# Three pairs of tiles transposed in 64-row halves, with the compute queues in a new order

## The chip, the cores and the metric

The kernel runs on one core of a Trainium2 chip. The metric is the device time of one execution in microseconds. TensorE multiplies into PSUM, which has eight banks; ScalarE and VectorE read PSUM, GpSimd does not; DMA queues are fed here from SyncE (SP). In profile lines the engines are PE (TensorE), PEld (its weight loads), ACT (ScalarE), DVE (VectorE), POOL (GpSimd) and SP.

## The reference

One transformer block on x of 2048 tokens and 448 features, all in bf16: a layer norm, an attention that is linear in the tokens ("hedgehog": softmax of plus and minus a learned projection as feature map), a residual, a second layer norm and a gated unit.

```
h  = x + A(layernorm(x));  out = h + B(layernorm(h))

A: q, k, v = split(x @ wqkv)                       # 16 heads of 28
   pq, pk = q @ w_phi, k @ w_phi                   # per head, 28 x 28
   phi(p) = concat(softmax(p), softmax(-p))        # 56 features
   kv  = sum over tokens of phi(pk)^T v;  z = sum over tokens of phi(pk)
   o   = (phi(pq) @ kv) / (phi(pq) . z + 1e-6)
   return o @ wo                                   # 448 x 448
B: return (sigmoid(x @ w_gate) * (x @ w_up)) @ w_down   # 448 -> 1792 -> 448
```

## The kernel before, in words

The 2048 tokens are 16 tiles of 128. Partition p of tile t holds token 16p + t, so a tile is one slice of `x_sb`. A matmul contracts over partitions, so three times a tile has to be turned so that features lie on partitions: the normed x (`xT`, into `xnT`), the attention's o (`oT`, into `oT`), and the normed h (`hT`, into `hnT`, which is the same memory as `xnT`). For most tiles a DMA transpose on SP's queue does it. For the tiles that come first in each stage TensorE does: x tiles 0 to 3, o tiles 0 and 1, h tiles 0 and 1. `pe_transpose` makes four 128 x 128 transposes of a tile into one bank (the 448 features lie in 512 padded columns), and `evac` copies the bank out on ScalarE or VectorE. Such an op is named `xT2`, its copy `xT2e`.

The contraction of 448 is done as seven blocks of 64 rows. Two 64-row halves of TensorE's array work at once, one for each of two banks (`pair`, `both`); after the first four steps (op `...a`) the halves change banks for the last three (op `...b`). The `a` and `b` op of one pair write the same banks from different halves, and where nothing lies between them the `b` op waits for the `a` op to end (`Graph.crosses`). Whole 128-row work is left in the warm-up multiplies (`warm0` to `warm9`), the folding of the weights (`wT`, `w2m`), these transposes, and the last down projections (`dm`).

The stages, in the order of time:

1. x arrives; statistics `bst`, `agg`; reciprocal root `pow1`; normed tile `xn`; its transpose `xT`. The weight fold for K (`w2m0`) and later for Q (`w2m1`, its copies `w2e1`).
2. For each tile: K features and V (`pva`, `pvb`; for tiles 0 to 3 `vva`, `vvb`, `ppa`, `ppb`, two tiles at a time), exponentials `ek` and V copy `v1_t` on ScalarE, the sums `ss`, their reciprocals `rs` and the products `phi` on VectorE or GpSimd, and the accumulation `kva`, `kvb` into banks 6 and 7. In between, Q features of the first chunk (`pqa`, `pqb`, exponentials `eq`; a chunk is four tiles).
3. `kvz` copies the accumulated kv out. `num` multiplies a tile's Q features with it; `rsm`, `qq`, `b`, `c`, `rden` on VectorE, `o` on GpSimd or VectorE; `oT`; the output projection `woa`, `wob`; the residual `h`; statistics (`bs2`, `ag2`, `pow2` for the first two tiles, `sq`, `ve`, `pow2` for the others); `hn`; `hT`.
4. The gates and ups (`ga`, `gb`; ScalarE `sig`, VectorE `hh`), two tiles at a time for tiles 0 to 3 and four at a time ("wide") from tile 4 on, and the down projections (`dn`, `dp`, later `dm`), `fin`, `out`. The attention of the later tiles runs among them.

The order of every engine is written out by hand in `ORDER`, one list of op names for each of sp, act, pe, dve and pool. Each engine executes its list in that order. Which engine executes an op that could run on several (`evac`, `xn`, `phi`, `o`, `hn`, `ve`, `nm`, `kvz`) follows from the list that holds its name. `Graph` finds from the keys that an op reads and writes (tiles, banks) which semaphores it has to wait for. `PROGRAM` sets only the order in which ops are declared.

Line 309 of the profile is the multiply in `both`, line 538 the transposes in `pe_transpose`, line 531 the copies in `evac`, line 612 the weight fold in `fold`, lines 671 and 672 the two exponentials in `ekv` (their tile `ek` lies in the memory of `hhT` and stands in the profile under that name), line 721 the exponentials in `pq`.

Of the kernel before, what the change touches and what calls it, by code (L numbers as in the profile page):

```python
# [18 lines left out]
class Graph:  # L19
# [90 lines left out]
    def emit(self, nc):  # L110
# [85 lines left out]
P = 128  # L196
# [5 lines left out]
KT = 4  # L202
# [123 lines left out]
def build(nc, A_x, A_wqkv, A_w_phi, A_wo, B_w_gate, B_w_up, B_w_down, out):  # L326
# [10 lines left out]
    with ExitStack() as es:  # L337
# [66 lines left out]
        def TS(t):  # L404
            return slice((t % 4) * P, (t % 4 + 1) * P)
# [126 lines left out]

        def pe_transpose(name, srcs, bank, dst, rkey, wkey):
            ps = bk16(bank)[:, 0:512]

            def f(e):
                for kt, src in enumerate(srcs):
                    p = e.transpose(ps[:, kt * P:(kt + 1) * P], src, ident[:])  # L538
                return p
            op("pe", name, f, r=["ident", rkey], w=[B(bank)])  # L540
            evac(name + "e", dst, ps.rearrange("p (k s) -> p k s", k=KT), B(bank), wkey)
# [22 lines left out]
        def xnorm(t, a):  # L564
            s = t % NX
            src = windows(x_sb[:, t, :])
            dst = xn_pad[:, s, :].rearrange("p (a f) -> p a f", a=2)

            def fa(e):
                return e.activation(dst, src, ACT.Identity, bias=nb1[:, t:t + 1], scale=rst1[:, t:t + 1])  # L570

            def fd(e):
                return e.tensor_scalar(dst, src, mv1[:, t, 0:1], rst1[:, t:t + 1], op0=ALU.subtract, op1=ALU.mult)

            def fp(e):
                return e.tensor_scalar(dst, src, nm1[:, t:t + 1], rst1[:, t:t + 1], op0=ALU.add, op1=ALU.mult)
            need = {"act": ("nb1", a), "pool": ("nm1", a), "dve": ("mv1", t)}[Graph.engine("xn%d" % t)]
            op(("act", "dve", "pool"), "xn%d" % t, (fa, fd, fp), r=[("x", t), ("rst1", a), need], w=[("xn", s)])
            if t < 4:
                pe_transpose("xT%d" % t, [xn_pad[:, s, kt * P:(kt + 1) * P] for kt in range(KT)], 6 + t % 2,  # L580
                             xnT[0][:, :, TS(t)], ("xn", s), ("xnT", t))
            else:
                op("sp", "xT%d" % t, lambda e: e.dma_start_transpose(out=xnT[t // 4][:, :, TS(t)], in_=xn_pad[:, s, :]),
                   r=[("xn", s)], w=[("xnT", t)], dma="tr", nring=64)
# [67 lines left out]
        def proj(t):  # L652
            bp, bv = t % 2, 2 + t % 2
            pairop("pva%d" % t, "pvb%d" % t, pair(bk(bp)[:, 0:D], bk(bv)[:, 0:D], x(t), x(t), wk2, wv),
                   [("xnT", t)] + W2k + wv_keys, bp, bv)

        def proj2(nm, t, b, w, r):
            pairop("%sa%d" % (nm, t), "%sb%d" % (nm, t), pair(bk(b)[:, 0:D], bk(b + 1)[:, 0:D], x(t), x(t + 1), w, w),
                   [("xnT", t), ("xnT", t + 1)] + r, b, b + 1)
# [51 lines left out]
        def pq(c, i, b):  # L711
# [3 lines left out]
            r = W2q + [("xnT", 4 * c + j) for j in range(4)]  # L715
# [101 lines left out]
        def otrans(t):  # L817
            so = t % NO
            if t < 2:
                pe_transpose("oT%d" % t, [o_pad[:, so, kt * P:(kt + 1) * P] for kt in range(KT)], 2 + t % 2, oT[:, so, :, :],  # L820
                             ("opad", so), ("oT", so))
            else:
                op("sp", "oT%d" % t, lambda e: e.dma_start_transpose(out=oT[:, so, :, :], in_=o_pad[:, so, :]),
                   r=[("opad", so)], w=[("oT", so)], dma="tr", nring=64)

        def resid(t, b, ha=False):
# [28 lines left out]
            if t >= 2:  # L855
                op("sp", "hT%d" % t, lambda e: e.dma_start_transpose(out=hnT[c][:, :, TS(t)], in_=hn_pad[:, s, :]),
                   r=[("hn", s)], w=[("xnT", t)], dma="tr", nring=64)

        def htrans(t):
            s = t % NH  # L860
            pe_transpose("hT%d" % t, [hn_pad[:, s, kt * P:(kt + 1) * P] for kt in range(KT)], t, hnT[0][:, :, TS(t)], ("hn", s), ("xnT", t))

        def wout(t):
# [14 lines left out]
            r = [("oT", t % NO), ("oT", (t + 1) % NO)] + wo_keys + ([("x", t), ("x", t + 1), "ident"] if ha else [])  # L878
# [5 lines left out]
        def wout1(t):  # L884
# [5 lines left out]
            r = [("oT", so)] + wo_keys  # L890
# [10 lines left out]
        def gate_up(t0, n, ff):  # L901
# [3 lines left out]
            hk = [("xnT", t) for t in range(t0, t0 + n)]  # L905
# [129 lines left out]
```

## Time and profile before

| | us |
|---|---|
| median of 3 runs | 202.45 (202.28 to 202.48) |
| the profiled execution's own time | 202.7 |
| its span, first to last instruction | 200.8 |
| TensorE busy | 195.5 (97%) |
| VectorE busy | 132.0 (66%) |
| ScalarE busy | 89.4 (45%) |
| GpSimd busy | 56.2 (28%) |

The granted TensorE clock is 1.000 over the whole span. A row of the timeline is: start, length, engine, line, operation, out<-in by the program's names, partitions of weights x columns, shape of the moving operand, how many; in brackets idle time of the engine before it and what ended that. Rows of TensorE overlap, since its multiplies are pipelined; the distance from one start to the next is what a piece of work takes of the engine. In the chain of waits a row is start, length and the work that held the chain. Times are microseconds from the span's start.

### The profile page before, as it was taken

Reading aid. Unit: us, or ns where it says so; the run is one execution under the profiler, and the core shown is the slowest. Engines: PE = TensorE matmul, PEld = TensorE weight load, DVE = VectorE, ACT = ScalarE, POOL = GpSimd, SP = SyncE. Lnnn points to the kernel's source line nnn. Section 1 sums busy time; section 2 is a strip of 40 time slices with the busy share of each in tenths; the row PEclk is TensorE's granted clock in tenths of the full one; section 3 lists DMA queues with packets and bytes.
Section 4 is the critical chain, followed back from the end, with each engine's and each line's share of the span. In section 5 each row is a group of like instructions: output and inputs, shape, how many; then the busy total and the mean of one; then the engine's idle time right before and its main releaser. Section 6 shows DMA issues by size and latency. Waiting matters only on the chain.

```text
span 200.8 us, 5854 instructions
## 1 busy us (share of the span) xinstructions
PE 195.5 (97%) x2516; PEld 114.4 (57%) x2516; DVE 132.0 (66%) x308; ACT 89.4 (45%) x174; POOL 56.2 (28%) x95
## 2 busy tenths in 40 slices
PE   7999999999999999999999999999999999999995
PEld 4835556565568778787444444555555555554443
DVE  5999999978888986576569877346332422272224
ACT  2668988898883451434232432324323212222220
POOL 5779948633343207510170110001400000000000
PEclk9999999999999999999999999999999999999999
DMA  6965346749984230360015220020312000004002
GB/s 157 316 140 129 54 83 76 221 144 302 309 206 66 52 57 15 66 82 3 0 29 124 56 42 10 20 58 26 65 38 52 0 3 2 0 3 137 0 3 91
DMA packets 32490, 16.26 MB, mean 81 GB/s; under 512 B 24720, under 2 KB 31568, under 8 KB 32464
## 3 DMA queue, kind: packets, MB, share of 16 engines
q1 hardware_dynamic: 32336, 15.86, 33.7%
q8 instruction: 20, 0.33, 0.7%
q14 instruction: 6, 0.05, 0.1%
q10 hardware_dynamic: 128, 0.03, 0.1%
HBM read 8.34 MB, written 1.84 MB: 51 GB/s over the span
## 4 chain that ended last, share of the span: by engine, by line
PE 92%; ACT 3%; DMA 2%; issue 1%; SPq 1%; DVE 0%
PE psum L309 84%; PE psum L954 5%; DMA wk_sb<-in_A_wqkv_dram 2%; ACT hhT L671 1%; ACT eq L721 1%; ACT hhT L672 1%; PE psum L524 1%; PE psum L538 1%; PE psum L612 1%; SPq L413 1%; PE psum L599 0%; ACT xnT L531 0%; ACT v L531 0%; DVE x_sb L961 0%
## 5 line engine op out<-in xcount | busy, mean ns | idle before, releaser
L309 PE MATMUL psum<-xnT,wu_sb 64*128 64x512 bf16 (+1 forms) x490 | 93.6, 333 | 0.0
L309 PE MATMUL psum<-xnT,wg_sb 64*128 64x512 bf16 (+1 forms) x490 | 93.5, 333 | 0.1
L925 ACT ACTIVATE sg_sb<-psum 128x512 bf16<-128x512 f32 x56 | 33.2, 596 | 90.1 <-PE psum L309 89.5
L926 DVE SCALAR_TENSOR_TENSOR hhT<-sg_sb,psum 128x512 bf16<-128x512 bf16 x56 | 37.7, 684 | 52.1 <-ACT sg_sb L925 51.7
L309 PEld LDWEIGHTS psum<-xnT,wg_sb 64*128 64x128 bf16 x490 | 44.6, 94 | 20.9 <-DVE hhT L926 2.5
L309 PEld LDWEIGHTS psum<-xnT,wu_sb 64*128 64x128 bf16 x490 | 44.7, 94 | 13.9
L309 PE MATMUL psum<-wd_sb,hhT 64*128 64x448 bf16 x336 | 37.3, 349 | 0.0
L309 PEld LDWEIGHTS psum<-wd_sb,hhT 64*128 64x128 bf16 x336 | 17.8, 94 | 14.2 <-DVE x_sb L836 0.5
L309 PE MATMUL psum<-Wk,xnT 64*128 64x448 bf16 x112 | 22.2, 350 | 0.5 <-ACT hhT L672 0.2
L309 PE MATMUL psum<-wv_sb,xnT 64*128 64x448 bf16 x112 | 22.3, 351 | 0.1
L810 POOL TENSOR_TENSOR o_pad<-c_sb,rden 128x448 bf16<-128x448 bf16 x11 | 10.2, 935 | 28.5 <-DVE rden L806 28.4
L675 DVE TENSOR_REDUCE ss<-hhT 128x32 f32<-128x896 bf16 x16 | 16.8, 1060 | 0.2 <-ACT hhT L672 0.2
L721 ACT ACTIVATE eq<-psum 120x1024 bf16<-120x1024 f32 x16 | 15.6, 1030 | 0.6 <-PE psum L309 0.4
L685 POOL TENSOR_TENSOR phi<-hhT,rs 128x896 bf16<-128x896 bf16 x8 | 13.6, 1710 | 5.6 <-DVE rs L681 3.4
L309 PE MATMUL psum<-xnT,Wq 64*120 64x512 bf16 x112 | 14.8, 383 | 0.3 <-ACT eq L721 0.2
L845 POOL TENSOR_SCALAR ve<-ssq 128x1 f32<-128x1 f32 x11 | 2.2, 201 | 41.8 <-ACT junk L842 41.5
L309 PE MATMUL psum<-wo_o,oT 64*128 64x448 bf16 x56 | 13.2, 350 | 0.0
L309 PE MATMUL psum<-wo_e,oT 64*128 64x448 bf16 x56 | 13.2, 349 | 0.0
L961 DVE SCALAR_TENSOR_TENSOR x_sb<-psum,x_sb 128x448 bf16<-128x448 f32 (+2 forms) x17 | 9.4, 592 | 2.9 <-PE psum L954 1.6
L954 PE MATMUL psum<-wd_sb,hhT 128*128 128x448 bf16 (+2 forms) x70 | 11.2, 316 | 0.0
L309 PEld LDWEIGHTS psum<-Wk,xnT 64*128 64x128 bf16 x112 | 7.8, 94 | 5.8 <-PE psum L309 1.0
L671 ACT ACTIVATE hhT<-psum 128x448 bf16<-128x448 f32 x16 | 8.8, 553 | 4.4 <-PE psum L309 4.2
(105 smaller groups left out, 234.4 us busy)
## 6 DMA issues: line engine op xcount, KB each, us to landing
out_dram<-x_sb SPq DMA_DIRECT2D x15, 112.0 KB, 1.8
x_sb<-in_A_x_dram SPq DMA_DIRECT2D x7, 224.0 KB, 4.2
wd_sb<-in_B_w_down_dram SPq DMA_DIRECT2D x7, 224.0 KB, 5.1
wg_sb<-in_B_w_gate_dram SPq DMA_DIRECT2D x3, 448.0 KB, 5.8
wu_sb<-in_B_w_up_dram SPq DMA_DIRECT2D x3, 448.0 KB, 5.7
wv_sb<-in_A_wqkv_dram SPq DMA_DIRECT2D x2, 224.0 KB, 4.7
wk_sb<-in_A_wqkv_dram SPq DMA_DIRECT2D x2, 196.0 KB, 4.1
wo_e<-in_A_wo_dram SPq DMA_DIRECT2D x1, 336.0 KB, 3.3
```

Of the source, the lines that this page charges most:

```text
L309: p = e.matmul(o, lhsT=w, rhs=r, start=st, stop=sp, tile_position=(row, 0))
L413: return op(eng, name, lambda e: e.dma_start(dst, src), r=r, w=w, dma="in" if eng == "sp" else "ain", nring=48 if eng == "sp" else 8, kb=kb)
L671: e.activation(ek[:, s, :, 0, :], src, ACT.Exp)
L675: op("dve", "ss%d" % t, lambda e: e.tensor_reduce(ss[:, s, :].rearrange("p (b h) -> p b h", h=2), eks.rearrange("p b (d h) -> p b h d", h= ...
L685: return e.tensor_tensor(phi[:, sp, :, :, :].rearrange("p b a n -> p (b a) n")[:, :, 0:56].rearrange("p b (d h) -> p b d h", h=2), eks.rea ...
L721: op("act", "eq%d_%d%s" % (c, i, "pm"[sg]), lambda e, sg=sg: e.activation(eq[c][:, sg, 2 * i:2 * i + 2, :].rearrange("p g n -> p (g n)"), ...
L810: return e.tensor_tensor(o_pad[:, t % NO, off:off + D].rearrange("p (h d) -> p h d", h=H), c_sb[:, t % NS, :, 0:DH], rden[:, t % NS, :][:, ...
L845: op(("pool", "dve"), "ve%d" % t, lambda e: e.tensor_scalar(ve2[:, t:t + 1], ssq2[:, t:t + 1], 1.0 / D ** 3, EPS, op0=ALU.mult, op1=ALU.ad ...
L925: op("act", "sig" + nm, lambda e: e.activation(sg_sb[:, k, 0:W], bk(bg)[:, 0:W], ACT.Tanh, scale=0.5), r=[B(bg)], w=[("sg", k)])
L926: op("dve", "hh" + nm, lambda e: e.scalar_tensor_tensor(out=dst, in0=sg_sb[:, k, 0:W].rearrange("p (f n) -> p f n", n=N), scalar=1.0, in1= ...
L954: p = e.matmul(bk(b)[:, lo:hi], lhsT=hb[:, ff, TS(t)], rhs=wd_sb[:, ff, lo:hi], start=ff == 0, stop=ff == FT - 1)
L961: op("dve", "fin%d%s" % (t, nm), lambda e: e.scalar_tensor_tensor(out=h_sb[:, t, lo:hi], in0=bk(b)[:, lo:hi], scalar=0.5, in1=h_sb[:, t, l ...
```

## The change

Tiles 2 and 3 of x, 0 and 1 of o, and 0 and 1 of h are transposed by one op for each pair (`xT2`, `oT0`, `hT0`), which stands where the second tile was declared. For each of the pair's eight 128 x 128 blocks it issues two transposes of 64 rows, one in each half of the array. The lower half writes one bank, the upper half the other: a bank holds one half of the tokens of both tiles, where it held all tokens of one tile. There are still two copies of 128 x 512 for each pair, which now write runs of 64 elements, and what reads one tile waits for both copies. So that this is tracked, the keys of `xnT` and `oT` are split by half (`XT`, `OT`).

The lists for act, pe, dve and pool have a new order up to about the gates of tiles 4 to 7. SP's list and `PACE` are as before. Ops also change engines: `xT3e` from act to dve, `oT1e` from dve to act, `o1` and `o4` from pool to dve, `o7` and `o8` from dve to pool, `phi8` from pool to dve and `phi5` from dve to pool, `v1_11` for `v1_13` on dve, `kvzA` for `kvzC` on dve, `nm1_6`, `nm1_8`, `nm1_12` from act to pool, `hn2`, `hn3` from dve to pool and `hn7` from pool to dve, and others of `ve`, `nm`, `o`.

```diff
+        def XT(t):
+            return [("xnT", t, 0), ("xnT", t, 1)]
...
+        def pair_transpose(names, srcs, banks, dst, rkeys, wkeys):
+            ps = [bk16(b)[:, 0:512] for b in banks]
+
+            def f(e):
+                for i, tile in enumerate(srcs):
+                    for kt, src in enumerate(tile):
+                        o = slice((i * KT + kt) * 64, (i * KT + kt + 1) * 64)
+                        for h, rows in enumerate((LO, HI)):
+                            p = e.transpose(ps[h][:, o], src[rows], ident[rows, rows], tile_position=(64 * h, 0))
+                return p
+            op("pe", names[0], f, r=["ident"] + rkeys, w=[B(b) for b in banks], rows=64, half={b: h for h, b in enumerate(banks)})
+            for h in range(2):
+                evac(names[h] + "e", dst[h], ps[h].rearrange("p (t k s) -> p t k s", t=2, k=KT), B(banks[h]), [k[h] for k in wkeys])
...
-            if t < 4:
+            if t in (2, 3):
+                if t == 3:
+                    v = xnT[0][:, :, 2 * P:4 * P].rearrange("p k (t h s) -> p h t k s", t=2, h=2)
+                    pair_transpose(("xT2", "xT3"), [[xn_pad[:, u % NX, kt * P:(kt + 1) * P] for kt in range(KT)] for u in (2, 3)], (6, 7),
+                                   [v[:, 0], v[:, 1]], [("xn", 2 % NX), ("xn", 3 % NX)], [XT(2), XT(3)])
...
+                    pair_transpose(("oT0", "oT1"), ..., (2, 3), [v[:, 0], v[:, 1]], [("opad", 0), ("opad", 1)], [OT(0), OT(1)])
...
+                    pair_transpose(("hT0", "hT1"), ..., (0, 1), [v[:, 0], v[:, 1]], [("hn", 0), ("hn", 1)], [XT(0), XT(1)])
```

The parts of the four lists that the prediction speaks of, before and after:

```diff
 act
-"... par ek0 xT3e ek1 v1_0 v1_1 nm1_6 ek2 ek3 v1_2 w2e1_1 v1_3 nm1_8 w2e1_0 v1_4 ek4 ..."
+"... par ek0 ek1 v1_0 v1_1 w2e1_1 ek2 v1_2 ek3 v1_3 w2e1_0 ek4 v1_4 ..."
-"... eq0_1m eq0_1p eq1_0p kvzA kvzB eq1_0m eq1_1p eq1_1m eq2_0m oT0e eq2_0p eq2_1m eq2_1p h1 h0 eq3_0p eq3_0m ..."
+"... eq0_1m eq0_1p eq1_0m kvzB kvzC eq1_0p eq1_1m eq1_1p eq2_0m oT0e oT1e eq2_0p eq2_1p eq2_1m h1 h0 eq3_0m eq3_0p ..."
 pe
-"... ppa0 ppb0 warm9 xT2 xT3 vva0 vvb0 ppa2 ppb2 vva2 seed vvb2 w2m1_0 w2m1_1 kva0 pva4 kvb0 pvb4 pva5 w2m1_2 w2m1_3 pvb5 ..."
+"... ppa0 ppb0 warm9 xT2 vva0 vvb0 ppa2 w2m1_1 ppb2 vva2 seed vvb2 w2m1_3 w2m1_0 pva4 pvb4 kva0 pva5 kvb0 kva1 pvb5 ..."
-"... pvb8 kvb3 pqb0_0 pva9 kva4 pvb9 pva10 kvb4 kva5 pvb10 kvb5 pva11 kva6 pvb11 ..."
+"... pvb8 kva3 pva9 kvb3 kva4 pvb9 pva10 kvb4 kva5 pvb10 kvb5 pva11 pqb0_0 kva6 pvb11 ..."
-"... qs pqa1_1 num0 num1 pqb1_1 pqa2_0 num2 pqb2_0 pqa2_1 oT0 oT1 num3 pqb2_1 woa0 wob0 ... num5 hT1 hT0 woa2 ga0_2 ..."
+"... qs pqa1_1 num0 pqb1_1 num1 pqa2_0 num2 pqb2_0 pqa2_1 oT0 pqb2_1 num3 wwo woa0 wob0 ... num5 hT0 woa2 ga0_2 ..."
 dve
-"... bst5 bst4 xn2 agg5 agg4 agg7 bst6 xT2e agg6 ss0 bst8 rs0 ..."
+"... bst5 agg7 bst4 xn2 agg5 agg4 bst9 bst6 xT3e xT2e agg6 bst11 ss0 bst10 rs0 ..."
-"... rsm2 rden1 qq2 b2 c2 oT1e rsm3 ... rsm5 hT1e qq5 hT0e b5 c5 ..."
+"... rsm2 rden1 qq2 o1 b2 c2 rsm3 ... rsm5 hT0e qq5 hT1e b5 rden4 c5 o4 ..."
 pool
-"... o0 o1 o2 o3 pow2_1 pow2_0 o4 o5 o6 ve2 ..."
+"... o0 o2 o3 pow2_1 pow2_0 o5 o6 ve3 o7 pow2_2 pow2_3 nm2 hn2 hn3 ..."
```

More of the change, by code (lines that the diff above doesn't have):

```diff
@@ L531, in evac, with OT @@
             op(("act", "dve"), name, (lambda e: e.copy(dst, src), lambda e: e.tensor_copy(dst, src)), r=[rkey], w=[wkey])
+        def XT(t):
+            return [("xnT", t, 0), ("xnT", t, 1)]
+        def OT(t):
+            return [("oT", t, 0), ("oT", t, 1)]
+        def pair_transpose(names, srcs, banks, dst, rkeys, wkeys):
[10 more added lines that the diff above has]
+                evac(names[h] + "e", dst[h], ps[h].rearrange("p (t k s) -> p t k s", t=2, k=KT), B(banks[h]), [k[h] for k in wkeys])
         def pe_transpose(name, srcs, bank, dst, rkey, wkey):
@@ L578, in xnorm @@
             op(("act", "dve", "pool"), "xn%d" % t, (fa, fd, fp), r=[("x", t), ("rst1", a), need], w=[("xn", s)])
-            if t < 4:
+            if t in (2, 3):
[3 more added lines that the diff above has]
+                                   [v[:, 0], v[:, 1]], [("xn", 2 % NX), ("xn", 3 % NX)], [XT(2), XT(3)])
+            elif t < 2:
                 pe_transpose("xT%d" % t, [xn_pad[:, s, kt * P:(kt + 1) * P] for kt in range(KT)], 6 + t % 2,
-                             xnT[0][:, :, TS(t)], ("xn", s), ("xnT", t))
+                             xnT[0][:, :, TS(t)], ("xn", s), XT(t))
             else:
                 op("sp", "xT%d" % t, lambda e: e.dma_start_transpose(out=xnT[t // 4][:, :, TS(t)], in_=xn_pad[:, s, :]),
-                   r=[("xn", s)], w=[("xnT", t)], dma="tr", nring=64)
+                   r=[("xn", s)], w=[XT(t)], dma="tr", nring=64)
         for ts in ([0], [1], [2], [3], [4, 5], [6, 7], [8, 9, 10, 11], [12, 13, 14, 15]):
@@ L654, in proj @@
             pairop("pva%d" % t, "pvb%d" % t, pair(bk(bp)[:, 0:D], bk(bv)[:, 0:D], x(t), x(t), wk2, wv),
-                   [("xnT", t)] + W2k + wv_keys, bp, bv)
+                   [XT(t)] + W2k + wv_keys, bp, bv)
         def proj2(nm, t, b, w, r):
             pairop("%sa%d" % (nm, t), "%sb%d" % (nm, t), pair(bk(b)[:, 0:D], bk(b + 1)[:, 0:D], x(t), x(t + 1), w, w),
-                   [("xnT", t), ("xnT", t + 1)] + r, b, b + 1)
+                   [XT(t), XT(t + 1)] + r, b, b + 1)
         def vcopy(t):
@@ L714, in pq @@
                           lambda h, k: xnT[c][h, k, :], lambda h, k: xnT[c][h, k, :])
-            r = W2q + [("xnT", 4 * c + j) for j in range(4)]
+            r = W2q + [XT(4 * c + j) for j in range(4)]
             op("pe", "pqa%d_%d" % (c, i), f1, r=r, w=[B(b), B(b + 1)], rows=64, half={b: 0, b + 1: 1})
@@ L819, in otrans @@
             if t < 2:
-                pe_transpose("oT%d" % t, [o_pad[:, so, kt * P:(kt + 1) * P] for kt in range(KT)], 2 + t % 2, oT[:, so, :, :],
-                             ("opad", so), ("oT", so))
+                if t == 1:
+                    v = oT[:, 0:2, :, :].rearrange("p t k (h s) -> p h t k s", h=2)
+                    pair_transpose(("oT0", "oT1"), [[o_pad[:, u, kt * P:(kt + 1) * P] for kt in range(KT)] for u in (0, 1)], (2, 3),
+                                   [v[:, 0], v[:, 1]], [("opad", 0), ("opad", 1)], [OT(0), OT(1)])
             else:
                 op("sp", "oT%d" % t, lambda e: e.dma_start_transpose(out=oT[:, so, :, :], in_=o_pad[:, so, :]),
-                   r=[("opad", so)], w=[("oT", so)], dma="tr", nring=64)
+                   r=[("opad", so)], w=[OT(so)], dma="tr", nring=64)
         def resid(t, b, ha=False):
@@ L856, in resid @@
                 op("sp", "hT%d" % t, lambda e: e.dma_start_transpose(out=hnT[c][:, :, TS(t)], in_=hn_pad[:, s, :]),
-                   r=[("hn", s)], w=[("xnT", t)], dma="tr", nring=64)
+                   r=[("hn", s)], w=[XT(t)], dma="tr", nring=64)
         def htrans(t):
-            s = t % NH
-            pe_transpose("hT%d" % t, [hn_pad[:, s, kt * P:(kt + 1) * P] for kt in range(KT)], t, hnT[0][:, :, TS(t)], ("hn", s), ("xnT", t))
+            if t == 1:
+                v = hnT[0][:, :, 0:2 * P].rearrange("p k (t h s) -> p h t k s", t=2, h=2)
+                pair_transpose(("hT0", "hT1"), [[hn_pad[:, u, kt * P:(kt + 1) * P] for kt in range(KT)] for u in (0, 1)], (0, 1),
+                               [v[:, 0], v[:, 1]], [("hn", 0), ("hn", 1)], [XT(0), XT(1)])
         def wout(t):
@@ L877, in fb @@
                             xp(t, 2, HI, False) + [(bk(2)[:, 0:D], ot(t)(HI, k), wo_e[HI, k, :], False, k == 2) for k in (0, 1, 2)])
-            r = [("oT", t % NO), ("oT", (t + 1) % NO)] + wo_keys + ([("x", t), ("x", t + 1), "ident"] if ha else [])
+            r = [OT(t % NO), OT((t + 1) % NO)] + wo_keys + ([("x", t), ("x", t + 1), "ident"] if ha else [])
             op("pe", "woa%d" % t, fa, r=r, w=[B(2), B(3)], rows=64, half={2: 0, 3: 1})
@@ L889, in part @@
                 return [(bk(b)[:, 0:D], oT[h, so, k, :], w[h, k, :], first and k == ks[0], not first and k == ks[-1]) for k in ks]
-            r = [("oT", so)] + wo_keys
+            r = [OT(so)] + wo_keys
             op("pe", "woa%d" % t, lambda e: both(e, part(LO, lo, True), []), r=r, w=[B(b)], rows=64, half={b: 0})
@@ L904, in gate_up @@
             ns = slice((t0 % 4) * P, (t0 % 4) * P + N)
-            hk = [("xnT", t) for t in range(t0, t0 + n)]
+            hk = [XT(t) for t in range(t0, t0 + n)]
             two = n == 2
```

65 rows, old and new, of the table ORDER are left out of this document.

## The prediction

> **What bounds the kernel now.** I read the page first, then the chain of waits, then the timeline of one engine at a time around each stall.
>
> ```profile
> span 200.8 us, 5854 instructions
> ```
>
> ```profile
> PE 92%; ACT 3%; DMA 2%; issue 1%; SPq 1%; DVE 0%
> ```
>
> TensorE carries nearly all of the chain that ends last. What an edit is worth is therefore the TensorE time that it takes away or adds, unless another engine makes TensorE wait at that place. The chain of waits (start, length, work) shows where that is so:
>
> ```profile
> 11.34 0.54 ACT hhT L671
> 11.88 0.43 ACT hhT L672
> 12.32 0.48 ACT xnT L531
> 12.79 0.45 ACT hhT L671
> 13.24 0.45 ACT hhT L672
> 13.69 0.14 issue
> 13.82 0.95 PE psum L309 x8
> 14.77 0.05 issue
> ...
> 17.45 0.43 ACT v L531
> 17.89 0.14 issue
> 18.02 2.49 PE psum L309 x30
> ...
> 47.20 1.95 ACT eq L721 x2
> 49.15 0.04 issue
> 49.19 1.07 PE psum L309 x8
> ```
>
> Three restarts of TensorE hang on ScalarE: ppa2 at 13.82 (behind ek0, the copy xT3e, and ek1), pva4 at 18.02 (behind v1_2), pqa2_1 at 49.19 (behind two exponentials). From 18 to 43 and from 59 to the end TensorE is on the chain almost alone. So 11 to 18 and 44 to 59 are the places to follow.
>
> **The transposes themselves.** TensorE's timeline at the three pairs, before:
>
> ```profile
> 11.23 0.29 PE L524 MATMUL psum<-zero 128*128 128x128 bf16 x2
> 11.35 0.61 PE L538 MATMUL psum<-ident,xn_pad 128*128 128x128 bf16 x8
> 11.89 1.74 PE L309 MATMUL psum<-wv_sb,xnT 64*128 64x448 bf16 x14
> ```
>
> ```profile
> 50.20 0.62 PE L538 MATMUL psum<-ident,o_pad 128*128 128x128 bf16 x8
> 50.75 0.40 PE L309 MATMUL psum<-kvz,eq 56*128 56x60 bf16 x16
> 50.99 0.84 PE L309 MATMUL psum<-xnT,Wq 64*120 64x512 bf16 x6
> 51.66 0.35 PE L309 MATMUL psum<-x_sb,ident 64*128 64x448 bf16 x2
> ```
>
> ```profile
> 57.59 0.62 PE L538 MATMUL psum<-ident,hn_pad 128*128 128x128 bf16 x8
> 58.14 0.36 PE L309 MATMUL psum<-wo_e,oT 64*128 64x448 bf16 x1
> ```
>
> Start to start, eight whole transposes and what follows them take 0.54 to 0.55. Two matrix multiplies of the same shape take 0.12 (11.23 to 11.35), at most 0.06 each, so eight take 0.45 to 0.48 and the change to 64-row work some 0.09. I take 0.09 for the change in the other direction too. No row shows a transpose in 64-row halves. The nearest is one `num`: 16 multiplies of 60 columns, alternating between the two row halves, take 0.24 (50.75 to 50.99), 15 ns each. Sixteen half transposes move 64 columns each, so 0.24 is my value and the lower end; the upper end is 16 at a whole transpose's 0.055 (0.44 divided by eight), 0.88. In the two later pairs the neighbours are 64-row work, so both changes of mode go as well: 0.55 + 0.09 - 0.24 = 0.40 of TensorE each. The first pair still stands behind `warm9`, whose rows are whole, and keeps one: 0.54 - 0.09 - 0.24 = 0.21. That is 1.01 us of TensorE. The question is how much of it meets a wait.
>
> The Trainium skill ("TensorE: Matmul & The Clock Gate", the section on 56 against 53.3 ns) says that starts of matmuls never come closer than about 25 ns, however few columns they have. By it a group of 16 takes 0.40 and not 0.24. The row at 50.75 disagrees, at 15 ns, but those are multiplies and not transposes; that case is the second rival.
>
> **Stage 1, 11 to 18 us.** The copy xT3e moves from ScalarE to VectorE, so ek1 ends 0.48 earlier (the L531 row of the chain), and ppa2 can start at 13.82 - 0.48 = 13.34. TensorE is ready then: half transposes 0.09 + 0.24 after 11.35, so the V projection starts at 11.68 instead of 11.89. Its row is 1.74 long, and the next work can start 0.16 before such a row ends (50.75 + 0.40 against 50.99), so 1.58 later, at 13.26. VectorE makes both copies:
>
> ```profile
> 11.78 0.42 DVE L531 COPY xnT<-psum 128x512 bf16<-128x512 bf16 x1
> ```
>
> bst9 now stands ahead of them, so they start about 12.2 and end by 12.2 + 2 x 0.42 = 13.04, before 13.34. Then the query fold w2m1_1 goes between ppa2 and ppb2. It fills the gap in which ppb2 waits for ppa2 to leave the banks: four pairs and the gap take 1.00 (13.82 + 0.95 + 0.05 - 13.82), seven pairs and the gap 1.58, so a pair takes 0.19 and the gap 0.23 to 0.24. The fold costs four multiplies, 0.20, and two changes of mode, 0.18: +0.15 here, taken back later, where one fold less runs. pva4 needs v1_2:
>
> ```profile
> 16.38 0.74 PE L309 MATMUL psum<-wv_sb,xnT 64*128 64x448 bf16 x6
> ```
>
> ```profile
> 17.31 0.57 ACT L531 CAST v<-psum 128x448 bf16<-128x448 f32 x1
> ```
>
> The V block that it reads ends at 16.38 + 0.74 - 0.48 + 0.15 = 16.79. v1_2 now stands ahead of ek3, so it starts with that: 16.79 + 0.04 + 0.57 + 0.14 to issue = 17.54, against 18.02. Stage 1: **-0.48**.
>
> **Stage 2, the K/V tiles to 44 us.** The new order of TensorE moves pqb0_0 and the kv steps so that other work lies in some of the gaps between a projection's two halves (about 0.12 each), and puts ScalarE's v copies closer to their users (I followed each tile's ek and v; three restarts come 0.1 to 0.2 late). I net this at +0.08. The danger is VectorE, which has no room:
>
> ```profile
> 30.00:35.00 5.00, 5.00 (x100) 3.14 (x98) 5.00 (x9) 4.33 (x11) 4.02 (x3) 1.00 0.60 70
> ```
>
> ```profile
> 42.22 1.14 DVE L685 TENSOR_TENSOR phi<-hhT,rs 128x896 bf16<-128x896 bf16 x2
> ```
>
> ```profile
> 43.69 0.76 PE L309 MATMUL psum<-v,phi 64*128 64x58 bf16 x24 [0.15 <-PE psum L309]
> ```
>
> Busy 5.00 of 5.00 (third pair of columns), its last two phi end at 43.36, and the block that uses the last one starts at 43.69. It gets one copy more (0.42, of which 0.08 overlaps). I expect it to win that back, because ek and the aggregates reach it 0.4 earlier and it stops waiting for them; if it wins nothing back, phi ends at 43.70 and stage 2 eats the whole gain (first rival). The moves between VectorE and GpSimd in this stage (phi5 for phi8, v1_11 for v1_13) swap equal shapes; their cover is the same slack of 0.3.
>
> **Stage 3, the o and h pairs, 44 to 59 us.**
>
> ```profile
> 49.99 0.64 DVE L804 TENSOR_TENSOR c_sb<-b_sb,psum 128x464 bf16<-128x464 bf16 x1
> ```
>
> ```profile
> L810 DVE TENSOR_TENSOR o_pad<-c_sb,rden 128x448 bf16<-128x448 bf16 x5 | 3.1, 625 | 0.1
> ```
>
> ```profile
> 50.63 0.58 ACT L531 COPY oT<-psum 128x512 bf16<-128x512 bf16 x1 [0.58 <-PE psum L538]
> ```
>
> In before's clock: num1 (0.24) now follows pqb1_1, so the exponentials of 47.20 start some 0.22 earlier and pqa2_1 starts at 48.97; it took 1.01 up to the transposes, 0.09 of it the change of mode, so it is done by 49.89. The pair waits for o1. o1 now runs on VectorE ahead of b2 and c2, when c1 and the small steps behind it are done at 49.2: 49.2 + 0.63 = 49.83, transposes 0.12 after that at 49.95, pqb2_1 at 50.19 (0.67 long, 50.99 to 51.66). b2 and c2 move by what of o1 their old waits don't absorb, 0.42: c2 ends at 50.63 + 0.42 = 51.05, and num3 waits to 51.18, a stall of 0.3 that was not there. Both copies are ScalarE's, one behind the other: 50.39 + 0.58 + 0.48 = 51.45, and woa0 starts at 51.55 against 51.66: **-0.11**. The 0.40 that the transposes gave up became waiting for the copies and c2.
>
> ```profile
> 55.60 3.77 ACT L721 ACTIVATE eq<-psum 120x1024 bf16<-120x1024 f32 x4
> ```
>
> ```profile
> 58.44 0.42 DVE L531 COPY xnT<-psum 128x512 bf16<-128x512 bf16 x1
> ```
>
> The h pair waits for banks that the second of these exponentials frees. The chain from woa0 to it moves by the same 0.11, so the pair starts at 57.48, and woa2 at 57.72 instead of 58.14. The gates wait for the second VectorE copy, though: it ends at 57.92 + 0.42 + 0.42 = 58.76 where it ended at 58.86. No gain beyond the 0.11.
>
> **Stage 4, after 59 us.** TensorE is full, and steps that change places (num9 to num11, dn0, ga2) do the same work.
>
> ```profile
> 57.48 0.94 POOL L810 TENSOR_TENSOR o_pad<-c_sb,rden 128x448 bf16<-128x448 bf16 x1 [1.08 <-DVE rden L806]
> ```
>
> ```profile
> oT<-o_pad SPq DMA_TRANSPOSE x14, 2.5
> ```
>
> o4, here on GpSimd, goes to VectorE behind c5, about 2 us later; its DMA transpose, and oT5's behind it on SP's queue, leave later too. The cover is sixteen gate steps ahead of woa4. hn2 and hn3 go the other way and delay theirs by about 1 us, with as much cover ahead of ga2_2. If a cover is gone, TensorE stands for the overhang, each landing 2.5 us after its issue. num10's c9 comes close, and I put +0.05 for that.
>
> **The sum.** -0.48 + 0.08 - 0.11 + 0.05 = -0.46. The profiled execution took 202.7 with a span of 200.8, so its own time would be 202.24, the span 200.34. It was 0.25 above the median of 202.45; on the median the forecast is **202.0**, -0.23%.
>
> **Rivals.**
> - *VectorE holds stage 2.* The extra copy isn't won back, kva15 starts no earlier than now, and stages 1 and 2 give nothing: -0.11 + 0.05, 202.4. For it: 5.00 of 5.00. Against: VectorE's own waits in this stage are for data that now come earlier. 0.14.
> - *The two row halves don't overlap, each half costing half a whole:* 16 x 0.0275 = 0.44, 0.20 over my value. The first pair has 0.08 of slack, the other two none: -0.46 + 0.12 + 0.40 = +0.06, 202.5. 0.07; the Trainium skill's floor of 25 ns would end in the same place.
> - *A half costs as much as a whole, one after the other* (the other side): 0.88 a group, 0.64 over. -0.46 + 0.56 + 1.28 = +1.38, 203.8. It decides from 26 ns a half transpose, where nothing is left; from 35 ns the kernel is slower by 0.2%. For it: transposes have only been seen whole, and their 64-row form isn't in this trace. Against: 15 ns in the `num` rows. 0.17, with everything between 35 and 55 ns.
> - *All of the freed TensorE time shows*: -0.48 and twice -0.40, 201.2. Against: the copies and exponentials above. 0.10.
>
> **How the numbers follow.** Forecast 0.52. A measurement of this kernel tells about 0.2% (0.4 us) from no change, and the forecast lies just past that: I put 0.37 of it beyond and 0.15 within. Faster: 0.37 + 0.10 = 0.47. Same: 0.15 + 0.14 + 0.07 = 0.36. Slower: 0.17. The forecast's own range is 201.7 to 202.3. 201.3 to 203.0 takes in the two middle rivals, most of the fast one and the near part of the slow one, and leaves out nearly 0.2.
>
> **What the profile after would show.** Right: 16 half transposes in about 0.24 before the next start; ppa2 at about 13.35, pva4 at 17.5; woa0 and the gates 0.5 earlier than before, with idle time on TensorE ahead of num3 and of the first gate that it did not have. Wrong: a group of 0.44 or more; a K/V block waiting for a phi of VectorE; pva4 no earlier than 17.9; a projection that waits for a DMA transpose; or the first gate 0.9 earlier, which would be the fast rival.

## The result and the profile after

| | before | after |
|---|---|---|
| median, us | 202.46 (6 runs, 202.14 to 202.81) | 206.39 (6 runs, 204.21 to 207.89) |
| ratio | | 1.0159, interval 1.0127 to 1.0192 |
| profiled execution, us | 202.7, span 200.8 | 204.82, span 203.0 |

The kernel became slower by 1.6%, against a forecast of 0.23% faster. One of after's six runs, 207.89 with a mean granted clock of 0.992, counts as slow and is left out of the ratio; the median of the other five is 205.9. The profiled execution is one of the quicker ones of after; it shows 2.2 us of the loss. Its page and its chain of waits:

```profile
span 203.0 us, 5897 instructions
...
PE 195.9 (97%) x2540; PEld 115.1 (57%) x2540; DVE 131.2 (65%) x307; ACT 89.9 (44%) x171; POOL 57.0 (28%) x99
...
q8 instruction: 20, 0.33, 0.7%
...
PE 91%; DVE 4%; DMA 2%; issue 1%; ACT 0%; DVEq 0%
```

TensorE has 24 multiplies and 24 weight loads more than before (2516 of each there). The shares by engine hide the change: the chain of before had 2% of DMA and 1% of "issue" too. Before, the 2% were the load of wk at 2.1 us; in after they are a transpose of o. In order of time:

```profile
16.88 0.54 ACT v L530
17.55 0.95 PE psum L308 x8
...
44.26 0.31 PE psum L308 x8
...
54.84 4.19 DMA oT<-o_pad
59.16 12.54 PE psum L308 x238
71.70 1.24 issue
72.94 52.95 PE psum L308 x722
```

From 54 us on there are two new links: a DMA transpose of o that took 4.19 us, and a hole of 1.24 in TensorE. TensorE's timeline names both places, and the three pairs:

```profile
11.56 0.41 PE L546 MATMUL psum<-ident,xn_pad 64*128 64x64 bf16 x16
11.81 1.73 PE L308 MATMUL psum<-wv_sb,xnT 64*128 64x448 bf16 x14
13.37 0.92 PE L308 MATMUL psum<-Wk,xnT 64*128 64x448 bf16 x8
```

```profile
50.13 0.41 PE L546 MATMUL psum<-ident,o_pad 64*128 64x64 bf16 x16
50.36 0.85 PE L308 MATMUL psum<-xnT,Wq 64*120 64x512 bf16 x6
51.26 0.40 PE L308 MATMUL psum<-kvz,eq 56*128 56x60 bf16 x16
51.79 0.37 PE L308 MATMUL psum<-x_sb,ident 64*128 64x448 bf16 x2
```

```profile
57.73 0.41 PE L546 MATMUL psum<-ident,hn_pad 64*128 64x64 bf16 x16
59.16 0.35 PE L308 MATMUL psum<-wo_e,oT 64*128 64x448 bf16 x1 [1.03 <-DMA oT<-o_pad]
...
72.94 0.35 PE L308 MATMUL psum<-wo_e,oT 64*128 64x448 bf16 x1 [1.24 <-issue]
```

Sixteen half transposes take 0.23 to 0.25 from their start to the next start, as forecast. Then woa2 (59.16) waits for oT3, 1.2 us longer than the 0.23 that the transposes ahead of it need, and woa6 (72.94) starts 1.5 us behind the last gate step (71.43), where those steps stand 0.11 apart, so it waits 1.4. The page puts the second hole down to "issue"; what came last there is oT7, issued at 68.63 and landed at 72.85, while h5, the other late thing that woa6 waits for, was done at 70.74. These two waits are 2.6 us; the span grew by 2.2.

The same transpose in the DMA view, in the window around it, before and after (packets, MB, share of 16 engines; KB each, us to landing):

```profile
q1 hardware_dynamic: 544, 0.13, 25.5%
issues: line engine op xcount, KB each, median us to landing
oT<-o_pad SPq DMA_TRANSPOSE x1, 2.4
```

```profile
q1 hardware_dynamic: 544, 0.13, 43.8%
q8 instruction: 1, 0.02, 2.1%
issues: line engine op xcount, KB each, median us to landing
oT<-o_pad SPq DMA_TRANSPOSE x1, 4.2
```

The transpose moves the same 0.13 MB, but takes 4.2 us for 2.4, and a packet of queue q8, kind "instruction", falls into its window. All 20 of these packets have 16,384 bytes, and they come about every 250 of TensorE's instructions: they are blocks of TensorE's own instruction stream being loaded. For oT2 and oT3 it is the same: a block is loaded from 56.00 to 57.49, and they land at 58.58 and 59.03, where before, with its nearest blocks at 50.8 and 58.9, they had landed at 56.84 and 57.24. There was little room: in before oT3 landed 0.9 us ahead of woa2 (58.14) and oT7 0.2 us ahead of woa6 (69.98).

### The profile page after: what moved, and what is told of

Same layout as the page of the kernel before. It is cut to its first block, busy times and chain, and to the rows that moved or that the text cites. A ratio compares the mean times of both kernels' runs of the same rounds, so it can differ in the third digit from the quotient of the medians.

```text
span 203.0 us, 5897 instructions
## 1 busy us (share of the span) xinstructions
PE 195.9 (97%) x2540; PEld 115.1 (57%) x2540; DVE 131.2 (65%) x307; ACT 89.9 (44%) x171; POOL 57.0 (28%) x99
## 4 chain that ended last, share of the span: by engine, by line
PE 91%; DVE 4%; DMA 2%; issue 1%; ACT 0%; DVEq 0%
PE psum L308 81%; PE psum L982 5%; DMA oT<-o_pad 2%; PE psum L523 2%; DVE c_sb L828 1%; DVE b_sb L825 1%; PE psum L490 1%; PE psum L636 1%; PE psum L623 1%; DVE st L855 0%; DVE kvz L774 0%; PE psum L557 0%; DVE o_pad L834 0%; ACT v L530 0%; PE psum L484 0%
## 5 line engine op out<-in xcount | busy, mean ns | idle before, releaser
L954 DVE SCALAR_TENSOR_TENSOR hhT<-sg_sb,psum 128x512 bf16<-128x512 bf16 x56 | 37.8, 686 | 54.7 <-ACT sg_sb L953 54.1
L308 PE MATMUL psum<-wv_sb,xnT 64*128 64x448 bf16 x112 | 22.8, 351 | 0.1
L834 POOL TENSOR_TENSOR o_pad<-c_sb,rden 128x448 bf16<-128x448 bf16 x10 | 9.3, 935 | 39.3 <-DVE rden L830 33.5
L825 DVE TENSOR_TENSOR b_sb<-psum,qq 128x464 bf16<-128x464 f32 x16 | 10.2, 636 | 0.7 <-PE psum L308 0.6
```

Of the source, the lines that this page charges most:

```text
L308: p = e.matmul(o, lhsT=w, rhs=r, start=st, stop=sp, tile_position=(row, 0))
L825: op("dve", "b%d" % t, lambda e: e.tensor_tensor(h3(b_sb), OMv[:, :, :, 0:EV], h2(qq)[:, :, :, None].to_broadcast([P, NB, 8, EV]), ALU.mul ...
L834: return e.tensor_tensor(o_pad[:, t % NO, off:off + D].rearrange("p (h d) -> p h d", h=H), c_sb[:, t % NS, :, 0:DH], rden[:, t % NS, :][:, ...
L954: op("dve", "hh" + nm, lambda e: e.scalar_tensor_tensor(out=dst, in0=sg_sb[:, k, 0:W].rearrange("p (f n) -> p f n", n=N), scalar=1.0, in1= ...
```

## The experiments

Theory P: a block of TensorE's instructions that is loaded while a DMA transpose is under way makes that transpose land 1 to 2 us late. The change adds 48 instructions and so moves the blocks onto oT3 and oT7, which have little slack. The rivals: H, the half transposes or what they set free cost the time; the order, the later o4 and o7 above all, has no cover left; W, the weight loads ahead of the transposes on SP's queue hold them up. In the first four expectations Q is the order and R is H, and in the first two P says less: what is lost lies in the DMA transposes that woa2 and woa6 wait for. One execution of each kernel was profiled.

### Taking the change apart

`e1_pairs_only` has the pair transposes and the orders and engines of before (xT3, oT1 and hT1 gone from pe's list).

> The pair transposes alone, with every queue in the order of before (xT2, oT0 and hT0 stand where the pairs stood). Theory P (the 64-row transposes work as forecast, and what is lost lies in the o transposes by DMA that woa2 and woa6 wait for): no loss, 201.7 to 202.6, each group about 0.24 us on TensorE. Rival Q (the new order is late by itself, whatever the DMA does): the same time here, 201.7 to 202.6. Rival R (the halves themselves cost): 203 or more.

`e2_order_only` has the orders of after with whole transposes:

```diff
-"... warm9 xT2 vva0 ... oT0 pqb2_1 ... hT0 woa2 ..."
+"... warm9 xT2 xT3 vva0 ... oT0 oT1 pqb2_1 ... hT0 hT1 woa2 ..."
```

> The new order alone, with whole 128-row transposes of each tile. Theory P: woa2 or woa6 still wait for oT2/oT3 and oT7, if the blocks of TensorE's instruction stream are loaded at the same places; with 48 TensorE instructions fewer ahead of them they are loaded up to 2 us later, so the two waits may be anything from 0 to 1.5 us: 202.5 to 206.5. Rival Q: 205 to 207 whatever the loads do. Rival R: 202.3 or less.

Measured: pairs only 204.51 (203.99 to 206.72), 1.011 [1.0071, 1.0148]; order only 202.53 (202.01 to 203.62), 1.0007 [0.9991, 1.0022]. The loss goes with the pairs, not with the order: o7 on GpSimd and o4 behind c5 cost nothing by themselves that these runs show. I had expected no loss from the pairs alone, and missed; 203 or more was what R said. In this kernel o7 stands on VectorE as before, and woa6 still finds its transpose late:

```profile
q1 hardware_dynamic: 555, 0.13, 15.9%
q8 instruction: 1, 0.02, 1.4%
issues: line engine op xcount, KB each, median us to landing
oT<-o_pad SPq DMA_TRANSPOSE x1, 4.0
```

That leaves two readings: the half transposes do it (H), or the 48 instructions do (P).

### Moving the blocks, with the work unchanged

The warm-up multiplies at the kernel's start read zeros and write a bank that nobody reads. Cutting them into other pieces changes TensorE's instruction count and not the work. `e3_after_shift` is after, `e4_before_shift` is before, both with 39 multiplies and 39 weight loads more:

```diff
-((4, 512), (1, 512), (1, 128), (2, 128), (1, 128), (6, 128), (4, 128), (6, 128), (8, 128), (2, 128))
+((16, 128), (4, 128), (1, 128), (2, 128), (1, 128), (12, 64), (8, 64), (12, 64), (16, 64), (2, 128))
```

> The changed kernel, with the warm-up multiplies cut into smaller ones: 39 more multiplies with 39 more weight loads at the start, about the same TensorE time, so that each later 16 KB block of TensorE's instructions is loaded some 78 instructions (about 3 us) earlier. Theory P (an instruction block that is loaded while a DMA transpose is under way makes that transpose late by 1 to 2 us): the loads at 56.0 and 69.9 move to about 53 and 67, oT3 lands before 58 and oT7 about 2.5 after its issue, the two waits of 1.0 and 1.2 us shrink to under 0.3, time 201.8 to 203.5. Rival Q: no change, 204 to 208.

> The kernel before, with the same 78 more TensorE instructions in the warm-up and nothing else. Theory P: the loads at 58.9 and 70.9 move to about 56 and 68, onto oT2/oT3 and oT7, and the kernel before gets the waits that the changed one has: 203.3 to 206. Rival Q, and anyone who holds the instruction stream for hidden: 202.2 to 202.8.

Measured: the changed kernel with 78 instructions more 202.49 (201.84 to 203.12), 0.9996 [0.9982, 1.001]; the kernel before with the same 78 more 204.20 (203.76 to 205.26), 1.0085 [1.0062, 1.0109]. The same addition takes the loss away from one and gives 0.85% to the other. In the shifted changed kernel blocks load at 53.8, 61.3 and 66.9. The first starts 1.0 behind the issue of oT2, which lands 3.7 after its issue; that is no later than in before (4.2, with no block but with the weight loads). oT3 and oT7 lie clear, and neither woa2 nor woa6 waits for o. The timeline at woa2:

```profile
57.38 0.41 PE L546 MATMUL psum<-ident,hn_pad 64*128 64x64 bf16 x16
57.63 0.35 PE L308 MATMUL psum<-wo_e,oT 64*128 64x448 bf16 x1
...
58.82 0.27 PE L308 MATMUL psum<-xnT,wg_sb 64*128 64x256 bf16 x1 [0.27 <-DVE xnT L530]
```

In the shifted kernel before, blocks at 54.8 and 68.7 meet oT3 and oT7, and TensorE waits 0.6 for each:

```profile
PE psum L309 <- issue: 0.6, 1, 0.6
PE psum L309 <- DMA oT<-o_pad: 0.6, 1, 0.6
```

`e5_before_plus48` gives the kernel before exactly the 48 instructions that the change adds (the same 6400 columns):

```diff
-... (1, 128), (6, 128), (4, 128), (6, 128), (8, 128), (2, 128))
+... (1, 128), (12, 64), (8, 64), (12, 64), (16, 64), (2, 128))
```

> The kernel before, whole transposes and its own orders, with the warm-up's 768, 512, 768 and 1024 columns cut into pieces of 64 instead of 128: 24 multiplies and 24 weight loads more, as many as the change adds, and no column more. Theory P (a block of TensorE's instructions that is loaded while a DMA transpose is under way makes that transpose land 1 to 2 us late): the blocks load as in the pairs-only kernel, one at about 56 us and one at about 69.8; o's third pair lands at 58 to 59, oT7 at about 71.5; woa6 waits about 1 us; 203.8 to 205.5, as the pairs-only kernel (204.5). Theory H (the half transposes themselves, by their work on TensorE, cost the time): nothing changes, 202.2 to 202.6.

Measured: 205.14 (204.61 to 207.0), 1.0153 [1.0114, 1.0192]. That is the loss of the whole change (1.0159) without a half transpose, a moved op or an added column. H isn't needed for it, and the kernels with fewer instructions below, which have the halves without the loss, exclude it. TensorE's waits from 50 to 75 us are close to those of after (1.2 and 1.0):

```profile
PE psum L309 <- issue: 1.3, 1, 1.3
PE psum L309 <- DMA oT<-o_pad: 1.2, 1, 1.2
```

Its profiled execution was one of the long ones (206.81), and shows where those lose more. xT10 to xT12 land 4.0 to 5.2 us after their issue (xT10 2.5 in before and after), with packets of instruction queues at 26.4 and 28.0 (q14, other engines) and at 29.97 (q8) among them. The K/V stage stops for xT11, and another hole, behind a phi of GpSimd, follows:

```profile
31.95 0.36 PE L309 MATMUL psum<-Wk,xnT 64*128 64x448 bf16 x1 [0.64 <-DMA xnT<-xn_pad]
...
36.84 0.29 PE L309 MATMUL psum<-v,phi 64*128 64x58 bf16 x8 [0.62 <-POOL phi L685]
```

What lengthens the long runs of after (206.88 to 207.89) is not shown: none of them was profiled. Delays like these are one candidate, the clock another: the runs of 206.88 and 207.89, and the longest ones of pairs only (206.72) and of this kernel (207.0), have a mean granted clock of 0.992, the run of 206.92 and the profiled 206.81 have 1.000.

### The other direction: fewer instructions

`e6_pairs_minus42` is pairs only, `e7_after_minus42` the changed kernel, both with 14 warm-up multiplies for 35:

```diff
+((4, 512), (1, 512), (1, 128), (1, 256), (1, 128), (1, 512), (1, 512), (1, 512), (2, 512), (1, 256))
```

> The pairs-only kernel (half transposes, orders of before) with the warm-up in 14 multiplies instead of 35 (5888 columns for 6400): 42 TensorE instructions fewer, six more than before in all. Theory P: blocks load near 58.5 and 71, clear of oT2, oT3 and oT7; no wait of woa2 or woa6 over 0.3; 201.8 to 202.6. Theory H: 204.5 as the pairs-only kernel.

> The changed kernel with the same shorter warm-up. Theory P: blocks load near 58.5 and 71; woa2 near 57.6, woa6 near 70.4, the span 200.3 to 200.6; 201.9 to 202.5. If oT7, which is issued at about 68 here, is still under way at the block near 71, woa6 waits up to 1 us and it is 203 to 203.5. Theory H: 206.4 as the changed kernel.

Measured: 202.31 (202.01 to 203.15), 0.9995 [0.9979, 1.0011], and 202.35 (202.0 to 203.45), 1.0006 [0.9985, 1.0027]. Both are cured of 2 to 4 us by 42 instructions fewer. The changed kernel's twelve runs fall into two groups, though: seven from 202.0 to 202.4, five from 203.2 to 203.5, and the profiled one is of the upper group. It has two holes that e3 doesn't have. At woa2 TensorE waits 0.49 for oT3. And ld_q2, a DMA transpose of weights issued at 9.97, lands at 14.77 (13.41 in after), and the query fold that the new order puts behind ppa2 waits for it:

```profile
13.09 0.93 PE L308 MATMUL psum<-Wk,xnT 64*128 64x448 bf16 x8
14.91 0.26 PE L636 MATMUL psum<-Wphi,WqT 112*128 112x112 bf16 x2 [0.89 <-DMA WqT<-in_A_wqkv_dram]
```

A block is loaded at 12.75 while ld_q2 is under way; that the block delays it is not shown, since with blocks at 12.86 (after) and 12.45 (e10, below) it lands at 13.41 and 13.12. In e6 ld_q2 is as late (14.70), but the order of before needs it only later, and nothing is lost.

`e9_pairs_minus38` and `e10_after_minus38` keep all 6400 columns, with 16 multiplies:

```diff
+((4, 512), (1, 512), (1, 128), (1, 256), (1, 128), (2, 384), (1, 512), (2, 384), (2, 512), (1, 256))
```

> The pairs-only kernel with the warm-up in 16 multiplies, all 6400 columns kept: 38 TensorE instructions fewer, ten more than before. Theory P: the phase of the kernel with 42 fewer (202.31), blocks near 57.4, 63.6 and 70.2, no wait of woa2 or woa6 over 0.3; the full warm-up takes away the runs of 203; span 200.2 to 200.4, 202.0 to 202.3. If the ten instructions already bring the block onto oT3, woa2 waits 0.5 and it is 202.5 to 203.

> The changed kernel with the same warm-up of 16 multiplies and 6400 columns. Theory P: woa2 near 57.7, woa6 near 70.4, span 200.4 to 200.6, 202.1 to 202.4, without the runs at 203.2 to 203.5 that the shorter warm-up had. The forecast of the prediction by itself would be 202.0.

Measured: 202.33 (201.94 to 203.2), 0.9994 [0.998, 1.0008], as expected; and 203.57 (203.06 to 205.31), 1.0069 [1.0044, 1.0093], which I had put at 202.1 to 202.4. The block that passed oT7 in the kernel with 42 fewer (issue 68.48, block 72.19, late by nothing) here comes at 69.23, 1.9 us behind oT7's issue at 67.31:

```profile
q1 hardware_dynamic: 544, 0.13, 14.8%
q8 instruction: 1, 0.02, 1.7%
issues: line engine op xcount, KB each, median us to landing
oT<-o_pad SPq DMA_TRANSPOSE x1, 4.2
```

```profile
58.59 11.85 PE psum L308 x230
70.44 1.19 issue
71.63 52.95 PE psum L308 x722
```

So a kernel next to one that is clear of oT7 has a hole of 1.19 there. P says why; it didn't let me say where the block would fall, to better than 2 us.

`e11_pairs_plus78` is pairs only with the shift of +78.

> The pairs-only kernel with the warm-up of the shifted changed kernel: 78 TensorE instructions more than pairs only, 126 more than before, 256 being a block. Theory P: blocks near 53.5, 61 and 66.5 as in the shifted changed kernel; oT2 late but landed by 56.7, oT3 and oT7 clear; woa2 and woa6 wait under 0.3; span 200.2 to 200.6, 201.9 to 202.5. A theory by which any added TensorE instruction costs by itself: over 205.

Measured: 202.72 (202.27 to 203.99), 1.0013 [0.999, 1.0035], above the 201.9 to 202.5 that I had expected. The block came at 54.6 and not 53.5, took 2.4 us beside the weight loads, and met oT3; woa2 waited 0.9 in the profiled execution, woa6 nothing. A cost for each added instruction (over 205) is excluded: 126 more than before cost 0.1%.

All fourteen kernels (e1 to e12 by their numbers) give one table for oT7, around which no weight load is under way (us; TensorE's hole is the idle time just before woa6):

| kernel | oT7 issued | nearest block starts | behind the issue by | landed after | hole |
|---|---|---|---|---|---|
| before | 67.37 | 70.92 | 3.6 | 2.4 | 0 |
| after | 68.63 | 69.88 | 1.3 | 4.2 | 1.24 |
| e1 | 67.92 | 69.76 | 1.8 | 4.0 | 1.30 |
| e2 | 67.55 | 71.19 | 3.6 | 2.4 | 0 |
| e3 | 67.54 | 66.87 | -0.7 | 2.4 | 0 |
| e4 | 67.74 | 68.66 | 0.9 | 3.3 | 0.64 |
| e5 | 70.14 | 72.12 | 2.0 | 4.0 | 1.29 |
| e6 | 66.83 | 70.27 | 3.4 | 2.4 | 0 |
| e7 | 68.48 | 72.19 | 3.7 | 2.4 | 0 |
| e8 | 67.51 | 69.43 | 1.9 | 4.0 | 0.16 |
| e9 | 66.73 | 70.31 | 3.6 | 2.4 | 0 |
| e10 | 67.31 | 69.23 | 1.9 | 4.2 | 1.19 |
| e11 | 67.98 | 67.63 | -0.4 | 2.4 | 0 |
| e12 | 67.02 | 71.38 | 4.4 | 2.4 | 0 |

Six blocks start 0.9 to 2.0 us behind the issue, and those six transposes land after 3.3 to 4.2; the other eight land after 2.4. No case is between.

The same count over all DMA transposes of the fourteen traces, of every stage, with no DMA other than transposes under way beside them, gives 27 more cases. All 33 with a block of TensorE starting 0.9 to 2.0 us behind the issue land after 3.3 to 4.5. All 175 with no instruction block of any engine from 1.2 us ahead of the issue to 2.5 us behind it land after 2.4 to 2.6. The shifted changed kernel, which loses nothing, has four of the 33: a late landing costs time only where something waits for it.

The traces also show which part is late. A block is one packet of 16,384 bytes. In e10 it lasts from 69.23 to 70.44, and all but two of oT7's 544 packets have begun by 69.35. The DMA view of the window from 69.36 to 71.6 has two packets of the transpose's queue:

```profile
q1 hardware_dynamic: 2, 0.00, 0.1%
```

These two begin at 70.43, as the block's packet ends. Fifteen of oT7's sixteen landings come at 69.57 to 69.71, in time; the sixteenth comes at 71.54. So it is in e1, e5 and e8: fifteen landings by 2.5 us after the issue, and one 1.0 to 1.2 us behind the end of the block. In after and e4, where the block starts earlier against the issue (1.3 and 0.9), all sixteen are late, the last 1.5 us behind its end.

### The weight loads

`e8_after_wd_late` is the changed kernel with its instruction count as it is:

```diff
 sp
-"... ld_wu3 ld_wd0 ld_wd1 ld_wd2 oT2 oT3 ld_wd3 ..."
+"... ld_wu3 oT2 oT3 ld_wd0 ld_wd1 ld_wd2 ld_wd3 ..."
```

> The changed kernel, its instruction count as it is, with the loads ld_wd0 to ld_wd2 issued behind oT3 instead of ahead of oT2, so that no weight load of theirs is in front of the two transposes. Theory W (o's third pair is late since it queues behind the weight loads): oT2 lands 2.5 us after its issue, oT3 by 57.4, woa2 at 57.7; woa6's wait, which has no weight load near it, stays; 204 to 205.5. Theory P: the block at 56 us still meets oT3, which lands at 58 to 59; woa2 waits 0.5 to 1 us, woa6 about 1.3; 205 to 207.

Measured: 203.59 (203.22 to 204.29), 1.0064 [1.0042, 1.0086]. Both theories' times were too high. With the weight loads gone oT3 lands at 57.29 and woa2 starts at 57.60, without a wait, though a block is loaded at 54.7. That fits W, but the block moved too: it starts 0.2 behind the issue of oT3, in after 1.2, so this run doesn't separate the two. But oT4, issued behind the moved loads with a block at 64.3, now lands 6.05 after its issue, and the wait has moved to woa4; oT7, with no load near it, is met by its block all the same (4.0):

```profile
65.97 0.27 PE L310 MATMUL psum<-xnT,wu_sb 64*128 64x256 bf16 x1
...
66.95 0.35 PE L310 MATMUL psum<-wo_e,oT 64*128 64x448 bf16 x1 [0.70 <-DMA oT<-o_pad]
```

`e12_pairs_m38_spread`, the try at a version ahead of both, is pairs only with 38 fewer and the loads of wd spread:

```diff
 sp
-"... ld_wu3 ld_wd0 ld_wd1 ld_wd2 oT2 oT3 ld_wd3 ld_wd4 ld_wd5 ld_wd6 oT4 oT5 ..."
+"... ld_wu3 oT2 oT3 ld_wd0 ld_wd1 ld_wd2 ld_wd3 oT4 ld_wd4 ld_wd5 ld_wd6 oT5 ..."
```

> The best version as the runs point to it: pairs only with 38 warm-up instructions fewer (202.33, its runs 201.94 to 203.2), and the loads ld_wd0 to ld_wd6 issued behind o's transposes oT2 and oT3 (four) and behind oT4 (three), where the first three stood ahead of oT2. Theory P with W as a second part (what is under way when a block or a queue of weight loads comes is late): oT2 and oT3 land 1 us earlier, oT5 at 64 to 66 as before, no wait of woa2, woa4 or woa6 over 0.3; the span 200.1 to 200.3 and 201.9 to 202.3, ahead of both kernels by 0.1 to 0.2%. Against it: oT4 and oT5 now stand behind four and three weight loads, and where a block meets them too, woa4 waits 0.3 to 0.9 as it did when the loads were moved in the changed kernel; 202.6 to 203.2.

Measured: 202.72 (202.05 to 203.67), 1.001 [0.9993, 1.0026]. oT2 and oT3 land at 55.36 and 56.43, 3.1 and 2.4 after their issue; with the loads ahead of them (e9) it was 4.6 and 3.3, in both kernels with no block starting from 0.5 us ahead of oT2's issue to oT3's landing. So W is a part of it: weight loads alone make these two land later. A block at 64.2 meets oT5, which is issued at 61.83 behind the loads and lands at 66.47, and woa4 has the hole of the doubt (0.43). No version that was run beats the kernel before by more than the interval.

## Why the prediction was wrong

**The step that failed** is stage 4: "If a cover is gone, TensorE stands for the overhang, each landing 2.5 us after its issue." I took the median of the page's row of DMA issues for a property of the transpose. For oT7 it is 2.4 when nothing meets it and 3.3 to 4.2 when a block of instructions does, and I priced no edit by the instructions that it adds to the stream. Before's own trace had landings of 4.2 for oT2 and 4.4 for oT4, so the median hid a spread that could have been read. The +0.05 that I put for stage 4 was 1.4 at woa6, and 1.2 at woa2, which waits for oT3 and which the sum took to follow hT0 at once. "A projection that waits for a DMA transpose" stood among the signs that would prove it wrong; none of the four rivals had it as its mechanism, and the slow one (a half costing a whole) was excluded by the first row; that its 203.8 lies nearest to the measured time is luck.

**Half transposes**: right. 0.25, 0.23, and hT0 to woa2 0.25 where oT3 is in time (57.38 to 57.63), against 0.24. By the rule of the Trainium skill ("TensorE: Matmul & The Clock Gate", the section on 56 against 53.3 ns) that starts come no closer than about 25 ns, an estimate for sixteen is 0.40; the rows disagree, at 14 to 16 ns each.

**Stage 1**: right. ppa2 at 13.37 (forecast 13.34), pva4 at 17.55 (17.54). That these times agree to 0.03 is luck in part, since the start of the span itself scatters: the last warm-up (`warm9`) starts at 11.23 in before, 11.35 in after, and 10.83 in the shifted kernel before (e4), which has the work of before. From `warm9` to pva4 it is 6.79 in before and 6.80 in e4, 6.20 in after and 6.31 in the shifted changed kernel: -0.59 and -0.48, for a forecast of -0.48.

**Stage 2**: mis-sized. kvb15 was to start 0.40 earlier than before (-0.48 + 0.08), at 43.77 for 44.17. It starts at 44.26 in after, where nothing of stage 1's gain is left. From pva4 to kvb15 it is 26.15 in before, 26.71 in after and 26.37 in the shifted kernel: +0.56 and +0.22 in place of +0.08. The order does the 0.22: with the orders of before it is 26.1 in e1, e6 and e9, which have the halves. Of the rest of after's 0.56, 0.3 comes at one kv step (42.58), and what that step waited for the profile doesn't name.

**Stage 3**: right in mechanism. From the transposes of o to woa0 I had 1.60, after has 1.66, with TensorE waiting for c2 (num3 starts 0.90 behind pqb2_1, whose work took 0.67 before) and for oT1e (woa0, 0.29), and the gates waiting for the second VectorE copy of h, as the row at 58.82 shows. The 0.40 of each later pair became waiting. The size was off: from kvb15 to woa0 it is 7.49 in before, 7.53 in after and 7.57 in the shifted kernel, so +0.04 to +0.08 in place of -0.11. woa0 starts at 51.79 in after and 51.66 in before, so the gain was gone before the two waits came.

**The sum without the blocks**: -0.46 was too much. The shifted kernel's span is 200.5 against 200.8 of before, so -0.3 in one execution of each. Order only also has 200.5, but its `warm9` starts 0.33 earlier; counted from there the halves bring 0.35 in that order. Over the runs nothing of this can be told apart (medians 202.49 and 202.53). The kernels that have the halves and no loss (e3, e6, e9) stand at 0.9994 to 0.9996, about -0.1 us, and their intervals take in 1. The fast rival (201.2) didn't come up either.

## What to carry to other kernels

In this kernel an edit that added instructions to an engine that is otherwise full moved every later load of its instruction stream, and this cost more than the work that was edited brought; before an edit is judged, run the kernel before with the same number of idle instructions added. A median time to landing is not a bound: for each DMA transpose that something on the chain waits for, read its own landing and how long before its user it comes. Here a block alone made landings 0.9 to 2.1 us later. And an improvement or a loss of one variant is only believed when it survives a shift of the instruction count.

## What the runs showed of the hardware

- TensorE's instructions come in 16,384-byte blocks over a queue of their own, 20 in a run of 5,080 recorded instructions, so some 254 each. A load takes 0.9 us at the least and up to 3.0 beside weight loads (e5, 56.3). The Trainium skill ("Runtime: NRT & Kernel Launch", Instruction fetch mechanics) has the blocks of 16 KiB and 256 instructions, and the traces agree. The Trainium skill (the same page and section) calls the cost of crossing a block mostly hidden. Here that holds for TensorE itself: in before, four blocks load between 50 and 75 us, and no wait of TensorE is listed there. It doesn't hold for the DMA transposes: 0.6 to 1.4 us for a single wait on a late transpose, 1.8 us for e4 and 3.4 for the five runs of after.
- A transpose that meets a block late in its course has one of its sixteen landings held until the block's packet has ended (e1, e5, e8, e10); one that meets it earlier lands late as a whole (all 16 of oT7 in after from 72.69 to 72.85). What stays open: why the held landing comes 1.0 to 1.5 us behind the end of the block, and what fixes the moment at which a block is asked for. e7 and e10 differ by four instructions and 512 warm-up columns, and the block's place against oT7 by 1.8 us; e6 and e9, by the same four and 512, and it hardly moves (3.4 and 3.6 behind the issue).
- The runs of after scatter by 2.7 us without the one of 207.89, those of the kernels without a loss (e3, e6, e9) by 1.1 to 1.3. e7 has two groups 1.0 apart. That a few tenths decide there whether a transpose is met would explain it, and is not shown, since one execution of each was profiled.
